# An ISAB attention with a SwiGLU feed-forward: a written list of block kinds, lent buffers and a listed opening

## Chip, cores and metric

The kernel runs on one core of one Trainium2 chip. The metric is device time in microseconds (us). TensorE, VectorE, ScalarE, GpSimd and SyncE are the engines; the profile calls them PE (its weight loads PEld), DVE, ACT, POOL and SP.

## What is computed

`x` has 4 batches of 12416 rows of 128 channels; there are 32 inducing points `I`.

```
mab(q, kv): softmax(q @ kv.T / sqrt(128)) @ kv
h  = mab(I, x)              # 32 rows for each batch
y  = mab(x, h)              # one row for each row of x
yn = y / rms(y) * rms_g
out = (silu(yn @ w_gate) * (yn @ w_val)) @ w_out      # 128 -> 1536 -> 128
```

Since `y = a @ h` with only 32 attention weights `a` for each row, the kernel never forms `y`. It multiplies `h` (scaled by `rms_g`) into the two first weight matrices once for each batch (the stacks `sg` and `sv`), and the rms norm follows from a 32 x 32 Gram matrix of `h`. The moving operand of the feed-forward part is `a`, split into a high and a low half so that a reduced-precision matmul (fp32r) loses nothing that matters: 4 x 32 rows fill the 128 partitions (high, low, high, low).

## The kernel before

**Tiling.** A batch is cut into 7 sets: five of 16 tiles of 128 rows, one of 15, one of 2. Set `s` has four units (quarters of its partitions), the last set one: 25 units to a batch, 20 of 512 columns, 4 of 480 and one of 256. A unit has 12 slots, one for each 128 of the 1536 hidden channels: 300 slots to a batch, 1200 in all.

**A slot** (`ffn.slot`, L674 to L701): a gate matmul (L677), Silu on ScalarE (L685), a value matmul (L688), their product on VectorE (L694). The product `u` then has to be multiplied with its piece of `w_out` and summed over the 12 slots. This is done in one of two ways.
- *plain*: one true fp32 matmul (`acc<-u,wo`, L613; it appears as two records).
- *three*: `u` is split into a high part, a scaled low part and their difference, and three fp32r matmuls (L633, L635, L613 with `more` or `xn` weights) take its place. There are two kinds. *sums*: one ScalarE (L659), one VectorE (L660) and one GpSimd operation (L669). *differences*: two ScalarE (L663, L668) and two GpSimd operations (L664, L669). Split tiles come from a ring of RING = 4 sets (`hi`, `lo`, `d`). The last two slots of a unit (j of 10 and 11) have no split weights and are always plain.

**Who decides.** The order on every engine is the order of the code: nothing is rescheduled. Before it emits the loop, the kernel rehearses it on a small model of its engines (`rehearse`). In `slot` of the rehearsal `decide` chooses the kind of each block by limits on how far an engine would fall behind in the next 8 slots (`fits`, LIMIT), and the filling of TensorE with ready projections is written down in `picks`. So each engine has one fixed order, and an instruction that waits holds everything behind it.

**Beside the slots** the next batch's attention is planned into slots (`schedule`): x loads, transposes, scores, softmax, weighted sums, stacks, second scores. A *seam* (L483) of 8 steps turns the attention weights of one set into `hi` and `lo` halves; `gather` (L537) copies them with DMAs from the SP queue into the moving tile `a` of a unit (4 DMAs of 64 KB).

**The opening** is written out by hand (L703 to L802). x and five of nine weight chunks are loaded; each weight chunk arrives as 64-bit floats and is rounded by `power`, `power_number`, `upper`, `upper_number`, `sign`, `lower` (VectorE, ScalarE, and one GpSimd multiply, after which a rounded `w_gate` or `w_val` chunk is stored to DRAM on SP, L221). Every x tile is transposed on TensorE (L313) and copied by ScalarE (L316), scored (L322, L326), and after a maximum over all sets (`max1` to `max3`) exponentiated (L355), transposed (L364) and summed (L378). Then come `divide`, `turn_h`, the scores of set 0, its softmax over rows, its seam and `spread`, which makes the moving tile of unit 0 on TensorE instead of by DMA, and the gathers of units 1 and 2. In the first 24 slots of batch 0, units 0 and 1 alternate in fours: slots 0 to 3 are unit 0, slots 4 to 7 unit 1. No three-way block is allowed in batch 0 before slot 26. `warm` (L183) emits TensorE fillers.

Of the kernel before, what the change touches and what calls it, by code (L numbers as in the profile page):

```python
# [23 lines left out]
def kernel(  # L24
# [73 lines left out]

    NK = NJ - 2
    RING, RESERVE, HELD, SILU = 4, 7, 9, 3  # L100

# [28 lines left out]
    def load_rows(b, s):  # L130

        n = per[s]
        t = xnat[b, s] = xnp.tile([P, 16 if b and n > 4 else n, C], F32, name=f"xn{s % 2 if b and n > 4 else s}")
        if b or s == full:
            for q in range(R):
                nc.sync.dma_start(out=t[ts(q, m), 0:n, :], in_=of(xrows, b, s)[q])
        else:
            d = xrows[ds(start[s], P * n), :].rearrange("(p t) c -> p t c", t=n)
            nc.sync.dma_start(out=t[:], in_=d)
# [34 lines left out]
    sel = up.tile([P, 512], F32R, name="u")[:, 0:2 * P].rearrange("p (k r c) -> p k r c", k=2, r=R)  # L174
    nc.gpsimd.memset(sel.bitcast(F32), 0.0)
    for k in range(R):
        nc.gpsimd.tensor_copy(out=sel[:, k % 2, k, :], in_=ident[:, 0:m])
# [36 lines left out]
    def rounding(i, c):  # L214
# [20 lines left out]
        def power():  # L235
# [12 lines left out]
            e = st["e"] = work.tile([P, 512], I32, name="we", tag="work")  # L248
# [25 lines left out]
        def lower():  # L274
            if wide:
                e, f = st["e"], st["f"].bitcast(F32)
                nc.vector.scalar_tensor_tensor(out=f[:], in0=st["low"].bitcast(U32), scalar=2.0 ** -52, in1=f[:],
                                               op0=ALU.mult, op1=ALU.add)
                nc.gpsimd.tensor_tensor(out=st["dst"], in0=f[:], in1=e.bitcast(F32)[:], op=ALU.mult)  # L279
            put()  # L280

# [8 lines left out]
    def attention(b, load_next):  # L290
# [9 lines left out]
        def turn_x(s, k):  # L300

            n = per[s]
            if b:
                t = xT[b, s]
                nc.vector.transpose(out=t[:, ts(k, n * m)], in_=t[:, ts(k, n * m)])
                return
            if not k:
                xT[b, s] = xtp.tile([P, R * n * m], F32, name=f"xT{s}")
            now = range(k * R, min(n, k * R + R))
            if now:  # L310
                ps = bank()
                for t in now:
                    nc.tensor.transpose(ps[:, ts(t - k * R, P)], xnat[b, s][:, t, :], ident[:])  # L313
                dst = xT[b, s][:].rearrange("p (q t i) -> p t q i", q=R, i=m)[:, now.start:now.stop, :, :]
                src = ps[:, 0:len(now) * P].rearrange("p (t q i) -> p t q i", q=R, i=m)
                nc.scalar.copy(out=dst, in_=src)  # L316
# [43 lines left out]
        def turn_e(s):  # L360
            e = st["e", s] = (once.tile([P, P], F32, name="hT") if b and per[s] < R else
                              work.tile([P, per[s] * m], F32, name="e", tag="work") if b else
                              up.tile([P, 512], F32, name="u"))[:, 0:per[s] * m]
            nc.vector.transpose(out=e, in_=sc[b][:, cols1[s]])  # L364

        def sum_h(*sets):

            hl = st["hl"]
            if b or not sets[0]:
                st["ps"] = bank()  # L370
            ps, whole = st["ps"], range(NS) if not b else sets
            tiles = [(s, t) for s in whole for t in range(per[s])]
# [6 lines left out]
            if b and sets[0]:  # L379
                nc.vector.tensor_tensor(out=hl[:, 0:C], in0=hl[:, 0:C], in1=ps[:, 0:C], op=ALU.add)  # L380
            elif b:
                nc.vector.tensor_copy(out=hl[:, 0:C], in_=ps[:, 0:C])
# [8 lines left out]
        def divide():  # L391
            st["hn"] = st["hl"][:, 0:C]
            nc.vector.tensor_scalar_mul(out=st["hn"], in0=st["hn"] if b else st["ps"][:, 0:C], scalar1=st["rl"][:])

        def turn_h():
# [5 lines left out]
            if b:  # L401
                scale_h()
# [5 lines left out]
        def square_h():  # L408

            if not b:  # L410
                scale_h()
# [3 lines left out]
            for q in range(R):  # L415
                to, of_ = gram[b][ts(q, m), ts(q, m)], ps[ts(q, m), 0:m]
                if b:
                    nc.vector.tensor_scalar_add(out=to, in0=of_, scalar1=C * 1e-6)
                else:
                    nc.scalar.activation(to, of_, AF.Copy, bias=C * 1e-6)  # L420

        def scores2(s, ps=None):
            ps = ps or scores(s, st["hT"][:, 0:m], quarters[s], per2[s])
# [40 lines left out]
        def stack_of(i, c):  # L464

            ps = st["stack", i, c] = bank()
            nc.tensor.matmul(ps[:], st["hg"][:], w0.pop((i, c)), start=True, stop=True)  # L467
            nc.scalar.copy(out=stacks[b][i][:, ts(c, 512)], in_=ps[:])
# [14 lines left out]
    def seam(b, s):  # L483

        st = {}
        n, rows = per2[s], rows2[s]
        w = n * m
        engine = nc.gpsimd if b or s else nc.vector
# [4 lines left out]
        def turn_a():  # L493
            eT = st["eT"] = work.tile([P, 512], F32, name="eT", tag="work")
            nc.vector.transpose(out=eT[rows, 0:w], in_=sc[b][rows, cols2[s]])
# [4 lines left out]

        def turn_z():
            ps = st["ps"]
            z = st["z"] = work.tile([P, n, m], F32, name="z", tag="work")
            flat = z[rows, :, :].rearrange("p t m -> p (t m)")
            nc.vector.tensor_tensor(out=flat, in0=ps[rows, 0:w], in1=st["eT"][rows, 0:w], op=ALU.mult)
            nc.vector.transpose(out=flat, in_=flat)

        def scale():
            ms = numbers("ms")
            nc.vector.reduce_sum(out=ms, in_=st["z"][rows, :, :], axis=AX.X)  # L510
            nc.vector.tensor_scalar(out=ms, in0=ms, scalar1=1.0 / C, scalar2=1e-6, op0=ALU.mult, op1=ALU.max)  # L511
            st["ms"] = ms
# [5 lines left out]
        def apply():  # L518
            rs, a = st["rs"], weights(b, s)
            engine.tensor_tensor(out=a, in0=a, in1=rs.unsqueeze(2).to_broadcast((rs.shape[0], n, m)), op=ALU.mult)  # L520

        def turn_b():
            aT = st["aT"] = work.tile([P, 512], F32, name="aT", tag="work")
            nc.vector.transpose(out=aT[rows, 0:w], in_=sc[b][rows, cols2[s]])

        def split():
            aT = st["aT"]
            hi, lo = split_of[b, s] = [halves.tile([P, 512], F32R, name=k) for k in ("hi", "lo")]
            if b or s:
                nc.scalar.copy(out=hi[rows, 0:w], in_=aT[rows, 0:w])  # L530
            else:
                nc.vector.tensor_copy(out=hi[rows, 0:w], in_=aT[rows, 0:w])
            engine.tensor_tensor(out=lo[rows, 0:w], in0=aT[rows, 0:w], in1=hi[rows, 0:w].bitcast(F32), op=ALU.subtract)

        return [turn_a, square, turn_z, scale, root, apply, turn_b, split]

    def gather(b, u):  # L537

        s, q = units[u]
        w = per2[s] * m  # L540
        hi, lo = split_of[b, s]
        a = moving[b, u] = (xnp.tile([P, 512], F32R, name="xn0") if (b, u) == (0, 2) else
                            astk.tile([P, 512], F32R, name="a"))
        for k, half in enumerate((hi, lo, hi, lo)):
            nc.sync.dma_start(out=a[ts(k, m), 0:w].bitcast(F32), in_=half[ts(q, m), 0:w].bitcast(F32))

    def spread(b, u):

        s, q = units[u]
        w = per2[s] * m  # L550
        hi, lo = split_of[b, s]
        assert not q and not flowing
        ps = bank()
        for k, half in enumerate((hi, lo)):
            nc.tensor.matmul(ps[:, 0:w], sel[:, k, :, :].rearrange("p k m -> p (k m)"), half[:, 0:w],
                             start=not k, stop=bool(k))
        a = moving[b, u] = astk.tile([P, 512], F32R, name="a")
        nc.scalar.copy(out=a[:, 0:w], in_=ps[:, 0:w])
# [7 lines left out]
    def split_wo(step):  # L566

        if not step:
            kws["first"] = xnp.tile([P, half + NK, C], F32R, name=f"xn{full - 1}")
            for name in ("hi", "lo", "d"):  # L570
                kws[name] = xnp.tile([P, RING, 512], F32R, name=f"xn{full - 4 + len(kws) - 2}")
# [23 lines left out]

    def weight_of(kind, j):
        n = kind * NK + j
        return kws["first"][:, n, :] if n < half + NK else kws["more"][:, n - half - NK, :]

    def ffn(b, u):  # L600
# [28 lines left out]
        def project3(j, hi, lo, d):  # L629
            if st["k"] == nk:  # L630
                st["u"] = ps_u.tile([P, 512], F32, name="u3")
            ups = st["u"]
            nc.tensor.matmul(ups[:, 0:T], weight_of(0, j), hi, start=st["k"] == nk, stop=False)  # L633
# [6 lines left out]
            kws["out"] -= 1  # L640

        def store(o):
            if s == full:
                d = out[ds(b * N + start[s], P * per[s]), :].rearrange("(i w) c -> i w c", i=m)
            else:
                d = of(out, b, s)[q]
            for k in range(R):
                queue = nc.scalar if (b, u) == flat[-1] and k % 2 else nc.sync
                queue.dma_start(out=d[:, :, ts(k, m)], in_=o[ts(k, m), 0:T].rearrange("p (t c) -> p t c", c=m))

        def three(j, t):

            assert kws.get("out", 0) < RING
            kws["out"] = kws.get("out", 0) + 1
            n = kws["n"] = (kws.get("n", 0) + 1) % RING
            hi, lo, d = (kws[name][:, n, 0:T] for name in ("hi", "lo", "d"))
# [9 lines left out]
            def rest():  # L666
# [3 lines left out]
                kara.append(lambda: project3(j, hi, lo, d))  # L670
# [41 lines left out]
    def parts(i, c, *engine):  # L712
        one = weight[i, c]
        one["power"]()
        one["power_number"](*engine)
        one["upper"]()
        one["upper_number"](*engine)

    def join(i, c):
        weight[i, c]["sign"]()  # L720
        weight[i, c]["lower"]()

    f["open_"]()
    warm(6)
    for s in range(NS):
        for k in range(R):
            f["turn_x"](s, k)

        for one in {0: (0,), 3: (1, 2), 4: (3, 4), NS - 1: (NS - 2,)}.get(s, ()):
            f["scores1"](one)  # L730
        if s == 4:
            parts(0, 0, nc.vector)
        if s == 5:
            join(0, 0)
    f["scores1"](NS - 1)
    one = weight[1, 0]
    f["max1"]()
    one["power"]()
    warm(4)
# [459 lines left out]
```

## Time and profile before

| | us |
|---|---|
| three runs | 1622.79, 1622.80, 1623.58 |
| profiled run, span | 1621.7 |
| L669, GpSimd, 705 operations | 870.9 |
| L664, GpSimd, 139 operations | 178.6 |
| L613 plain, TensorE, 990 records | 490.8 |
| first gate matmul starts | 55.48 |

The page gives the busy time of each engine, the chain that ended last, and the costliest groups of instructions. In a timeline a line is the start, the duration, the engine, the source line and operation, the tiles (written `<-` read), the shape and the number of instructions that were merged; in square brackets stands the idle time before and what ended it. Matmuls are pipelined: their durations overlap, and the distance between two starts is what one costs.

Two things about the opening are read from the timeline of VectorE: from 20 us on it is busy most of the time, and the weights' rounding stands in the same queue as the attention chain. The last loads of x land at about 22 us.

### The profile page before, as it was taken

What the parts mean: (1) busy time and instruction counts of PE and PEld (TensorE: products, weight loads), DVE (VectorE), ACT (ScalarE), POOL (GpSimd) and SP (SyncE); (2) the same over time, 40 slices, a digit from 0 to 9 for tenths busy, and PEclk for the clock granted to TensorE, in tenths of its full rate; (3) what the DMA queues carried; (4) which work ended last, traced back from release to release, by engine and by line L of the source; (5) the groups of instructions that cost most, each with busy time, mean ns of one, the idle gap of its engine ahead of it and who ended that gap; (6) DMA issues with size and microseconds to landing.
All of it is one profiled execution on the core that took longest, in us unless ns stands there. A gap on an engine that the chain in (4) does not pass through costs nothing.

```text
span 1621.7 us, 25435 instructions
## 1 busy us (share of the span) xinstructions
PE 1604.3 (99%) x7085; PEld 1085.6 (67%) x7085; DVE 1444.6 (89%) x2504; ACT 1238.3 (76%) x2285; POOL 1217.7 (75%) x979
## 2 busy tenths in 40 slices
PE   8999999999999999999999999999999999999998
PEld 6546666756676666766677666676667777777776
DVE  4879988999899998899899998789989999999997
ACT  4567877767887778776778777877778888878886
POOL 1358885878588886688678888587858878878876
PEclk9999999999999999999999999999999999999999
DMA  7455624444353141634445323353221122111221
GB/s 262 91 72 85 112 43 97 88 97 69 60 94 59 36 95 29 133 76 81 69 67 83 55 54 68 63 125 79 46 38 29 31 39 40 35 35 36 40 38 26
DMA packets 389181, 112.52 MB, mean 69 GB/s; under 512 B 365072, under 2 KB 369712, under 8 KB 386480
## 3 DMA queue, kind: packets, MB, share of 16 engines
q1 hardware_dynamic: 388304, 110.82, 34.8%
q8 instruction: 56, 0.92, 0.3%
q14 instruction: 85, 0.70, 0.2%
q10 hardware_dynamic: 736, 0.08, 0.0%
HBM read 53.95 MB, written 27.00 MB: 50 GB/s over the span
## 4 chain that ended last, share of the span: by engine, by line
PE 94%; DVE 1%; ACT 1%; issue 1%; POOL 0%; DVEq 0%; ACTq 0%
PE acc L613 35%; PE gv L677 18%; PE gv L688 16%; PE u L635 10%; PE u L633 10%; PE gv L322 3%; PE gv L499 1%; PE gv L378 1%; DVE gv L694 1%; ACT silu L685 1%; PE gv L453 0%; DVE xn L660 0%; PE gv L467 0%; DVE o L621 0%; POOL xn L279 0%
## 5 line engine op out<-in xcount | busy, mean ns | idle before, releaser
L669 POOL TENSOR_TENSOR xn<-xn,xn 128x512 fp32r<-128x512 f32 (+2 forms) x705 | 870.9, 1255 | 268.6 <-DVE xn L660 156.8
L685 ACT ACTIVATE silu<-gv 128x512 f32<-128x512 f32 (+2 forms) x1186 | 689.7, 586 | 258.4 <-PE gv L677 231.8
L688 PE MATMUL gv<-a,sv 128*128 128x512 f32 (+2 forms) x1188 | 636.1, 536 | 0.8 <-ACT silu L685 0.8
L613 PE MATMUL acc<-u,wo 128*128 128x512 f32 (+1 forms) x990 | 490.8, 581 | 0.0
L677 PE MATMUL gv<-a,sg 128*128 128x512 f32 (+2 forms) x1188 | 486.7, 410 | 1.5 <-ACT silu L685 0.8
L694 DVE TENSOR_TENSOR u<-silu,gv 128x512 f32<-128x512 f32 (+2 forms) x621 | 407.7, 663 | 51.7 <-PE gv L688 32.3
L694 DVE TENSOR_TENSOR gv<-silu,gv 128x512 f32<-128x512 f32 (+2 forms) x565 | 376.0, 668 | 66.1 <-PE gv L688 49.0
L660 DVE SCALAR_TENSOR_TENSOR xn<-xn,gv 128x512 fp32r<-128x512 f32 (+2 forms) x566 | 371.3, 656 | 9.5 <-ACT xn L659 5.9
L659 ACT ACTIVATE xn<-gv 128x512 fp32r<-128x512 f32 (+2 forms) x566 | 330.4, 584 | 43.1 <-DVE gv L694 30.9
L677 PEld LDWEIGHTS gv<-a,sg 128*128 128x128 f32 x1188 | 223.8, 188 | 189.4 <-ACT silu L685 40.2
L688 PEld LDWEIGHTS gv<-a,sv 128*128 128x128 f32 x1188 | 223.6, 188 | 139.6 <-issue 46.3
L613 PE MATMUL acc<-xn,more 128*128 128x512 f32 (+2 forms) x705 | 273.6, 388 | 3.0 <-DVE o L621 2.6
L633 PE MATMUL u<-xn,xn 128*128 128x512 f32 (+2 forms) x705 | 272.4, 386 | 0.0
L613 PEld LDWEIGHTS acc<-u,wo 128*128 128x128 f32 x990 | 184.9, 188 | 46.7 <-issue 9.1
L664 POOL TENSOR_TENSOR xn<-u,xn 128x512 fp32r<-128x512 f32 (+2 forms) x139 | 178.6, 1285 | 41.6 <-ACT xn L663 41.6
L635 PE MATMUL u<-xn,xn 128*128 128x512 f32 (+2 forms) x414 | 160.1, 387 | 0.0
L613 PEld LDWEIGHTS acc<-xn,more 128*128 128x128 f32 x705 | 132.4, 188 | 33.5 <-POOL xn L669 5.7
L633 PEld LDWEIGHTS u<-xn,xn 128*128 128x128 f32 x705 | 132.6, 188 | 28.6 <-issue 5.5
L663 ACT ACTIVATE xn<-u 128x512 fp32r<-128x512 f32 (+2 forms) x139 | 87.4, 629 | 36.6 <-DVE u L694 32.4
L635 PE MATMUL u<-xn,more 128*128 128x512 f32 (+2 forms) x291 | 112.5, 387 | 0.0
L516 POOL TENSOR_TENSOR rs<-ms,mhalf 128x16 f32<-128x16 f32 (+2 forms) x28 | 75.9, 2709 | 18.1 <-DVE ms L511 17.1
L635 PEld LDWEIGHTS u<-xn,xn 128*128 128x128 f32 x414 | 77.7, 188 | 17.5 <-DVE gv L694 0.2
(151 smaller groups left out, 1096.9 us busy)
## 6 DMA issues: line engine op xcount, KB each, us to landing
out_dram<-o SPq DMA_DIRECT2D x320, 64.0 KB, 2.0
xT<-in_x_dram SPq DMA_DIRECT2D x60, 256.0 KB, 5.4
xn<-in_x_dram SPq DMA_DIRECT2D x60, 256.0 KB, 5.0
a<-hi SPq DMA_DIRECT2D x156, 64.0 KB, 2.0
a<-lo SPq DMA_DIRECT2D x156, 64.0 KB, 2.0
xn<-in_x_dram SPq DMA_DIRECT2D x5, 1024.0 KB, 10.6
xn<-w SPq DMA_DIRECT2D x18, 256.0 KB, 3.6
out_dram<-o SPq DMA_DIRECT2D x64, 60.0 KB, 2.0
```

The lines of the kernel that those rows point to most:

```text
L613: nc.tensor.matmul(acc[:, 0:T], lhsT, rhs, start=st["left"] == NJ, stop=st["left"] == 1)
L633: nc.tensor.matmul(ups[:, 0:T], weight_of(0, j), hi, start=st["k"] == nk, stop=False)
L635: nc.tensor.matmul(ups[:, 0:T], weight_of(1, j), lo, start=False, stop=not st["k"])
L659: nc.scalar.activation(hi, v, AF.Copy, scale=(1.0 - 2.0 ** -13) * 2.0 ** -12)
L660: nc.vector.scalar_tensor_tensor(out=lo, in0=hi.bitcast(F32), scalar=-4096.0, in1=v, op0=ALU.mult, op1=ALU.add)
L663: nc.scalar.activation(d, v, AF.Copy, scale=1.0 - 2.0 ** -13)
L664: nc.gpsimd.tensor_tensor(out=lo, in0=v, in1=d.bitcast(F32), op=ALU.subtract)
L669: nc.gpsimd.tensor_tensor(out=d, in0=hi.bitcast(F32), in1=lo.bitcast(F32), op=ALU.subtract)
L677: nc.tensor.matmul(g[:, 0:T], sg[:, ts(j, P)], a[:, 0:T], start=True, stop=True)
L685: nc.scalar.activation(sl[:, 0:T], g[:, 0:T], AF.Silu)
L688: nc.tensor.matmul(v[:, 0:T], sv[:, ts(j, P)], a[:, 0:T], start=True, stop=True)
L694: nc.vector.tensor_tensor(out=t[:, 0:T], in0=sl[:, 0:T], in1=v[:, 0:T], op=ALU.mult)
```

## The change

1. **Kinds of blocks.** `decide`, `fits`, LIMIT and the table of loads go. The kinds stand in a list of 900 letters (`s`, `d`, `.`), 300 each for batch 0, for batches 1 and 2 together, and for batch 3. In batch 3 slots 10 and 11 may be three-way as well: `split_last` makes their split weights in the buffer `xT0`.
2. **Lent buffers.** The ring of four sets becomes a list of free sets, and two more sets are cut out of the second pair of stack buffers (`sg`, `sv`), which is idle between two batches: lent at slot 20 (batch 0) or 2, called back at slot 184, gone at 192. In batch 3 they stay.
3. **Some prices** of the rehearsal change (for instance `sum_h` 1.85 to 2.0), and it knows when the accumulator bank of an older unit is free.
4. **The opening** is cut into some 200 named steps that stand in one listed order. The softmax of the inducing points over the rows of x has three groups of sets with a maximum each, (0,1,2), (3,4), (5,6); their sums are brought together by factors exp(difference of maxima). Six of the copies of transposed x go to VectorE. The load of set 5 is cut in two DMAs.
5. **Set 0 in two halves.** The scores are split into halves of 8 row tiles. The seam of the first half is in the opening, that of the second is planned into slots 5 to 15. Units 0 and 1 are now made of the first half of all four quarters and units 2 and 3 of the second, so a gather for these is 8 DMAs of 32 KB and a store 8 instead of 4. Of the gathers only that of unit 1 stays in the opening; that of unit 2 goes to slot 18. The weight chunks (0,1) and (1,1) are finished in the opening, at the end of the list, ahead of the gather.

The core of the diff:

```diff
+    GROUPS = ((0, 1, 2), (3, 4), (5, 6))
+    HALF = 8
+    ORDER = """
+        tx03 cp03v tx00 tx02 tx01 cp00 cp01 cp02v sc0 tx12 tx13 tx10 cp12v cp13v tx11 ev0 tx23 cp11v tx21 tx60 cp10
...
+        te5 rec pn10 p11 su4 shs dv0 su5 sg20 dv1 su6 dv2 th lw20 hT sg10 s2A gp gr0 hg tnA gr2 rmxA subA gr3 s2B w6
+        jn20 lw10 pn11 e2A ta u01 gr1 sq tnB z jn10 so00 tz rz ms rmxB ca00 so10 w12 un01 u11 sl00 subB pow ap un11
+        ca10 e2B silu tb hi sp1 lo sl10 sg01 sg11 sp2 cpa lw01 jn01 gate lw11 jn11
+    """
+    LENT = (RING, RING + 1)
...
+    def lend(b, k, idle, leaving):
+
+        if k == (20 if not b else 2):
+            idle += LENT
+            return True
+        if b + 1 < B and k == 184:
+            leaving += [n for n in LENT if n not in idle]
+            idle[:] = [n for n in idle if n not in LENT]
+        assert k != 192 or not leaving
...
+    def lend_tiles():
+
+        tiles = [stk.tile([P, F], F32R, name=name) for name in ("sg", "sv")]
+        kws["sets"][RING:] = [[t[:, ts(n, 512)] for n in range(3)] for t in tiles]
...
     gather(0, 1)
-    gather(0, 2)
-    weight[0, 1]["lower"]()
     flowing.append(True)
...
-            add(0, weight[1, 1]["sign"])
-            add(1, weight[1, 1]["lower"])
-            for k, one in ((1, (2, 1)), (5, (0, 2)), (8, (1, 2)), (11, (2, 2))):
+            for k, one in ((0, (2, 1)), (5, (0, 2)), (8, (1, 2)), (11, (2, 2))):
...
+            for k, step in zip((5, 6, 8, 9, 10, 13, 14, 15), seam(0, 0, 1)):
+                add(k, step)
+            add(18, gather, 0, 2)
...
+        if b + 1 == B:
+            for step in range(3):
+                add(2 + 2 * step, split_last, step)
...
-    LIMIT = (0, 0.8, 0.8, 2.6)
     kinds, picks = {}, {}
+    letters = """
+        ..........................d....dsd...d..s.dd.s..dss.ssdssd..dssssddd.d..ss..dsdd....dsds.d.ss...sds.
...
+    BLOCKS = [letters[NU * NJ * n:NU * NJ * (n + 1)] for n in (0, 1, 1, 2)]
...
-            kind = decide(b, k, u, j)
+            kind = {"s": "sums", "d": "differences"}.get(BLOCKS[b][k])
```

In the list, the letters name a step and the digits its set or weight chunk: `tx`/`cp` transpose and copy (a final `v`: on VectorE), `sc`/`ev` scores and their eviction, `m1` to `m3` the maximum, `ex`/`te`/`su` exponential, transposition and sum, `dv` the division, `th`/`hT` the transposed `h`, `s2`, `tn`, `rmx`, `sub`, `e2` the scores and softmax of a half (A, B), `ta` to `lo` the seam of the first half, `sp` and `cpa` the spread, `w` fillers; `p`, `pn`, `u`, `un`, `sg`, `lw`, `jn` the rounding of a weight chunk, `so`, `ca`, `sl` a stack.

## The prediction

> **What bounds the kernel now.** I read the page first (busy shares, chain of work that ended last), then the timeline of TensorE in the steady part, then the chain in order of time, and last the timeline around the first matmul of the feed-forward part.
>
> ```profile
> PE 1604.3 (99%) x7085; PEld 1085.6 (67%) x7085; DVE 1444.6 (89%) x2504; ACT 1238.3 (76%) x2285; POOL 1217.7 (75%) x979
> PE 94%; DVE 1%; ACT 1%; issue 1%; POOL 0%; DVEq 0%; ACTq 0%
> ```
>
> TensorE is busy almost throughout and is 94% of the chain. A busy TensorE need not be a full one, so I price its work by the distance between starts:
>
> ```profile
> 331.99 0.40 PE L677 MATMUL gv<-a,sg 128*128 128x512 f32 x1
> 332.22 1.02 PE L613 MATMUL acc<-u,wo 128*128 128x512 f32 x2
> 332.68 0.79 PE L688 MATMUL gv<-a,sv 128*128 128x512 f32 x1
> 333.31 0.40 PE L677 MATMUL gv<-a,sg 128*128 128x512 f32 x1
> 333.54 0.40 PE L633 MATMUL u<-xn,xn 128*128 128x512 f32 x1
> 333.78 0.39 PE L635 MATMUL u<-xn,xn 128*128 128x512 f32 x1
> 334.01 0.39 PE L613 MATMUL acc<-xn,more 128*128 128x512 f32 x1
> 334.24 0.40 PE L688 MATMUL gv<-a,sv 128*128 128x512 f32 x1
> ```
>
> Gate to gate with one plain fp32 projection is 333.31 − 331.99 = 1.32 us. A reduced matmul takes 0.23, so plain costs 1.32 − 2 x 0.23 = 0.86. The same projection as three reduced matmuls takes 334.24 − 333.54 = 0.70. Converting a block of 512 columns therefore saves TensorE 0.16 us; of 480 columns 0.15 and of 256 about 0.08, in proportion.
>
> With these prices the work after the opening is: gate and value matmuls 960, 192 and 48 pairs (512, 480, 256 columns), 542 us; 705 three-way blocks (567, 105, 33), 476; 495 plain ones, 414; attention inside the loop about 96 (the rows of L322, L378, L453, L499, L467). Together 1528 us, against 1561 from the first gate matmul at 55.48 to the last projection at about 1616.9. So about **33 us are gaps**. One batch repeats every 394.1 us (first lines of the second scores of the next batch, chain in order of time):
>
> ```profile
> 334.63 0.99 PE gv L322 x8
> ...
> 728.77 0.99 PE gv L322 x8
> ...
> 1122.95 1.00 PE gv L322 x8
> ```
>
> The opening is another regime: TensorE runs fillers (L183) and a chain over VectorE, ScalarE and GpSimd sets the start:
>
> ```profile
> 53.55 0.62 SPq L545 DMA_DIRECT2D a<-hi  x1
> 53.55 0.69 DVE L533 TENSOR_TENSOR lo<-aT,hi 128x512 fp32r<-128x512 f32 x1
> 55.47 0.58 SPq L545 DMA_DIRECT2D a<-lo  x1
> 55.48 0.50 PE L677 MATMUL gv<-a,sg 128*128 128x512 f32 x1
> 58.69 0.53 SPq L221 DMA_DIRECT2D w<-xn  x1
> 59.51 0.39 PE L677 MATMUL gv<-a,sg 128*128 128x512 f32 x1
> ```
>
> Unit 0 starts at 55.48, 1.24 us after `lo` is finished at 54.24. Unit 1 starts with slot 4 at 59.51; its four gathers had been issued by 56.05 and, at 2.0 us to landing, were there at about 57.5. The store of the rounded weight chunk (L221) stands behind them in SP's queue.
>
> **What the skill says.** *FP8 and Floating Point Precision*, TensorE Precision Notes: true fp32 takes four passes, reduced fp32 reads 4 bytes and truncates. The trace agrees: 0.86 is nearly four times 0.23. *SBUF — State Buffer*, Who interferes with whom: VectorE and GpSimd share one port pair, and a VectorE instruction with two SBUF inputs or in a 2-port mode blocks. The trace agrees in the opening: L249 at 44.42 took 0.90 us beside GpSimd's multiply (43.77, 1.27 us), and 0.43 at 50.15. In the steady part VectorE's L694 and L660 have one operand in PSUM, so by that page they leave the pair alone. *GPSIMD Engine Reference*, Engine selection, puts two-input elementwise work at about twice VectorE's time; here 1.29 (L533 on GpSimd, 512 columns) against 0.69.
>
> **Part 1: the list of kinds.** The letters hold 556 sums and 230 differences, 786 three-way blocks, against 566 + 139 = 705. By width: 634, 114, 38 against 567, 105, 33. Saving on TensorE: 67 x 0.1625 + 9 x 0.15 + 5 x 0.08 = **12.7 us**; the engine bounds, so it goes to the end. The price is paid elsewhere. GpSimd gets 81 + 91 = 172 more operations; from the row `3.56 us x3` at 799.06 one 480-column operation repeats every 1.17, so 1.25 at 512: about +207 us. ScalarE gets 91 x 2 x 0.63 − 10 x 0.58 = +108, VectorE −10 x 0.66. GpSimd goes to about 1430 of 1605 (89%), ScalarE to 84%, VectorE stays at 90%. All below TensorE on average, so I charge nothing to the sum, but dense units exceed it: unit 5 of batch 0 (9 blocks, 5 differences) asks 14 x 1.25 = 17.5 us of GpSimd in about 14.4 of TensorE. The two lent sets (six instead of four) let that queue up. Their effect on gaps is not visible before: bounded by −10 (batches 0 to 2 come down to the 1.2% of gap that I count in batch 3) and +10 (a wait of 0.013 us per block). I take −3, since six sets make the waits for a free one rarer. The three small weight splits of the last batch (3 ScalarE operations at 0.38 and 2 GpSimd at 0.73, by the 256-column rows of L659 and L669) hide beside its slots.
>
> **Part 2: the opening.** The last x set lands at 22.1 (issued 4.5, 17.6 to landing), in both. Before, its chain waits for one maximum over all sets (bias at 29.8), four exponentials (to 33.7), transposes (to 36.3). After, only sets 5 and 6 are left then. VectorE, in order, decides. Its queue from the first copy at 8.8 to the last score eviction holds 17 us, and that eviction's data come at about 26: end at 26 to 28.7, say 27.5. From there the listed order gives: 24 instructions to `hT` (transposes 0.65, two-input 0.60, tensor_scalar in SBUF 0.34, small ones 0.12 to 0.35) 8.0; sign, scaling and the scores of the half set 0.9; the half chain (256-column steps 0.44 each as in 1572.96 to 1573.39, lw10, u01, tnB, then a power of 8 columns, 1.63 by the 32x8 row of L516, under which rmxB, u11, sl00, subB lie) to the end of `lo` 7.9; two port locks by the multiplies jn20 and jn10, 0.9 each. `lo` ends at 27.5 + 18.6 = **46**, the first gate at 47.3: 8.2 earlier.
>
> But not all of that is kept. The built order shows on SP, ahead of the gathers of unit 1: the store of jn01, a raw load, the store of jn11. After `lo` VectorE does sl10, sg01, sg11, lw01, lw11 (5 x 0.61), GpSimd jn01 and jn11 (1.28 each, the first behind lw11 by the port): jn11 ends at `lo` + 5.7. Then the store (0.53), then **eight** gathers of half width at 0.63 apart (as 53.55 to 58.00 shows) instead of four: last issue at + 10.7, landing 1.8 later: + 12.5, about 58.5. Slot 4 needs it and TensorE's order is fixed, so TensorE stands from about + 6 to + 12.5. Slot 4 starts at 58.5 against 59.51: **1 us earlier, not 8**. VectorE has caught up by then (before, slot 4's product ran at 62.88, 3.4 after its gate; now 0.9 after), but gets the second half's seam in slots 5 to 15 (0.42 + 0.79 + 0.54 + 0.42 = 2.2, GpSimd 2.9, ScalarE 0.35, TensorE 0.05). I take −2 for the opening, bounds −8 (the gathers don't hold) and +1.
>
> **Part 3: the end.** The last unit has differences up to slot 9; the chain of two ScalarE and two GpSimd steps (0.4 and 0.73 at 256 columns) is partly beside the last plain products: +0.3.
>
> **Sum.** 1621.7 − 12.7 − 3 − 2 + 0.3 = 1604.3; the other runs lie 1.1 above the profiled span (1622.8): **1605**.
>
> **Rivals.**
> 1. The gathers of unit 1 don't hold slot 4 (they land in time or other work fills in): the opening keeps its 8.2, and 1622.8 − 12.7 − 3 − 8.2 + 0.3 = **1599**. For it: slots 0 to 3 need jn01 as well (their weight product so01), so slot 4 may be late whatever the gathers do, and only the difference counts; against it: one in-order queue and the issue times above. 19%.
> 2. GpSimd's higher share turns into waits at the reduced projections: gaps grow by 6 instead of falling by 3, **1614**. For it: dense units above 100%. Against it: six sets, and only 5.7 us of waits of weight loads on L669 now. 20%.
> 3. GpSimd becomes the bound: **slower**. All its work after 75 us is 982 block operations (in units of 512) x 1.25 + 157 = 1385 us, which ends at 1460. If port conflicts made one operation cost more than 1.42, it would end at 1625 or later; at 1.43, **1636**. Against it: the median is 1.287, the maximum 1.330. 8%.
> 4. The gain of part 1 is eaten exactly: 1623. 3%.
> My own case, 50%, spans 1599 to 1611. A measurement tells about 0.2% from no change. The range takes in rivals 1 and 2: 1593 to 1617. Faster 0.89, same 0.03, slower 0.08.
>
> **What would show it.** Right: 786 three-way blocks; about 390 us from batch 1 to 2; the first gate near 47; a TensorE idle of about 6 us before the gate of slot 4, released by a DMA; gaps about 30. Wrong: slot 4 at 52 with no wait (rival 1); weight loads waiting long on the GpSimd subtraction (rivals 2, 3); VectorE much later than 46 with `lo`, for which I counted port locks only twice.

## The result and the profile after

The changed kernel takes **1640.5 us** (median of 4 runs, 1639.5 to 1641.8) against 1622.8: a ratio of 1.0108, 95% interval 1.0096 to 1.0120. It is slower, and the forecast was 1605. From the page of the changed kernel, its busy times, its chain by engine and its clock row (PEclk, the TensorE clock that was granted, in tenths of full speed):

```profile
PE 1595.6 (97%) x7100; PEld 1092.9 (67%) x7100; DVE 1458.7 (89%) x2519; ACT 1301.2 (79%) x2457; POOL 1425.9 (87%) x1160
PE 86%; DVE 4%; ACT 3%; DMA 2%; issue 2%; POOL 1%; SPq 1%; POOLq 0%; DVEq 0%; ACTq 0%
PEclk8899999999999999999999999999999999999999
```

GpSimd's 1425.9 us are the 1430 that the forecast worked out. TensorE's share of the chain fell from 94% to 86%, and its clock row now begins with two slices below the rest. The chain in order of time shows where the loss is not (first lines of the second scores of the next batch):

```profile
351.69 1.00 PE gv L332 x8
...
746.44 1.00 PE gv L332 x8
...
1142.31 1.00 PE gv L332 x8
```

A batch takes 394.8 and 395.9 us, no less than before (394.1 and 394.2); 390 had been forecast. But the first of these lines stands 17.1 us later than before. So two things need an explanation: an opening that loses some 18 us, and 81 more three-way blocks that bring next to nothing.

The timeline of the opening, TensorE first:

```profile
21.81 2.37 PE L804 MATMUL gv<-ident,xn 128*128 128x128 f32 x10 [8.77 <-DMA xn<-in_x_dram]
51.98 0.67 PE L506 MATMUL gv<-eT,gram 128*128 128x256 f32 x2 [3.23 <-DVE eT L502]
59.87 0.50 PE L750 MATMUL gv<-a,sg 128*128 128x512 f32 x1 [0.68 <-ACT a L591]
71.14 0.76 PE L750 MATMUL gv<-a,sg 128*128 128x512 f32 x1 [5.83 <-DMA a<-lo]
71.70 1.91 PE L685 MATMUL acc<-u,wo 128*128 128x512 f32 x2
72.62 1.41 PE L761 MATMUL gv<-a,sv 128*128 128x512 f32 x1
```

TensorE stands 8.8 us for an x load, 3.2 for VectorE's `eT`, and 5.8 for a gather. The first gate is at 59.87 (before 55.48), the one of slot 4 at 71.14 (before 59.51). After the stand a pass of a plain projection takes 72.62 − 71.70 = 0.92 us, where it took 332.68 − 332.22 = 0.46 in the steady part. The Trainium skill, *TensorE: Matmul & The Clock Gate*, Part 1, says that an idle array falls to half its clock until it has been busy for a few microseconds; the factor of two after a stand of 5.83 us agrees. The window from 71 to 77 us (busy us of TensorE, its weight loads, VectorE, ScalarE and GpSimd with their instruction counts; then the clock as a share of full speed, the DMA share, GB/s) has it directly, a clock of 0.52:

```profile
71.00:77.00 6.00, 5.86 (x10) 3.01 (x10) 1.29 (x2) 1.68 (x3) 0.00 (x0) 0.52 0.90 135
```

VectorE in the same stretch:

```profile
25.97 0.69 DVE L816 TENSOR_SCALAR_CACHE_REDUCE sc<-gv 128x512 f32<-128x512 f32 x1 [12.61 <-PE gv L332]
37.23 0.66 DVE L816 TENSOR_SCALAR_CACHE_REDUCE sc<-gv 128x480 f32<-128x480 f32 x1 [0.41 <-PE gv L332]
50.79 0.69 DVE L293 SCALAR_TENSOR_TENSOR o<-sc,o 128x512 f32<-128x512 uint32 x1 [2.08 <-DMA sc<-in_moe_w_gate_dram]
51.76 1.35 DVE L278 TENSOR_SCALAR o<-sg 128x512 int32<-128x512 int32 x1
58.01 0.43 DVE L552 TENSOR_TENSOR lo<-aT,hi 128x256 fp32r<-128x256 f32 x1
74.14 0.69 DVE L767 TENSOR_TENSOR u<-silu,gv 128x512 f32<-128x512 f32 x1 [6.25 <-PE gv L761]
```

It is idle for 12.6 us behind TensorE's stand and waits 2.1 us for a raw weight chunk at `lw10` (L293). The two port locks that the forecast counted are there (L287 at 45.54 and L278 last 1.71 and 1.35, beside GpSimd's multiplies). The last score eviction (480 columns, set 5) ends at 37.9 and not at 27.5, `lo` at 58.44 and not at 46. While TensorE stands for the gather, VectorE has nothing left to do and waits 6.25 us.

SyncE's queue (SPq) between `lo` and slot 4:

```profile
62.84 0.33 SPq L236 DMA_DIRECT2D w<-xn  x1
63.26 0.38 SPq L224 DMA_DIRECT2D sg<-in_moe_w_out_dram  x1
64.26 0.33 SPq L236 DMA_DIRECT2D w<-xn  x1
64.64 0.62 SPq L577 DMA_DIRECT2D a<-hi  x1
...
69.11 0.59 SPq L577 DMA_DIRECT2D a<-lo  x1
```

This is what the forecast described: store, raw load, store, eight gathers. Slot 4 starts at `lo` + 12.7; + 12.5 had been forecast, with a stand of about 6 before it where 5.83 is seen.

The following table is worked out from the timelines of TensorE: the start of the n-th gate matmul less that of the kernel before, in us, and the same for the end of the span. All later sections use it. Each row is one profiled run and can differ from the medians: that of the mended opening took 1621.3 us, 1.3 above its median, that of the kernel before 1623.6, 0.8 above.

| kernel | gate 0 | 4 | 26 | 200 | 300 | 600 | 900 | end |
|---|---|---|---|---|---|---|---|---|
| after | 4.4 | 11.6 | 18.6 | 17.1 | 17.5 | 19.5 | 20.1 | 18.3 |
| new opening, kinds of before | 4.9 | 12.1 | 19.3 | 20.9 | 21.2 | 23.3 | 25.2 | 25.6 |
| set 6 last | −5.9 | 1.3 | 8.6 | 7.0 | 7.6 | 8.5 | 9.3 | 7.4 |
| gather first | 5.8 | 7.3 | 11.5 | 9.9 | 10.4 | 11.2 | 11.9 | 9.3 |
| mended opening | −7.6 | −6.1 | −0.3 | −1.8 | −1.3 | −0.4 | 0.3 | −2.2 |
| + gather of unit 2 earlier | −8.4 | −7.0 | −4.5 | −6.0 | −5.2 | −4.3 | −3.7 | −6.2 |
| + places earlier | −8.1 | −6.6 | −4.2 | −5.8 | −5.1 | −6.3 | −7.6 | −9.1 |
| new kinds, old opening | −0.9 | −0.9 | −0.9 | −2.4 | −1.7 | −2.1 | −2.6 | −5.2 |
| new kinds in the last batch only, old opening | −0.9 | −0.9 | −1.0 | 2.4 | 2.6 | 5.0 | 7.2 | 5.4 |
| new kinds, GpSimd narrow | −0.6 | −0.6 | −0.6 | −2.0 | −1.2 | −4.3 | −7.5 | −10.0 |
| new kinds, VectorE narrow | −0.7 | −0.7 | −0.7 | −2.1 | −1.3 | −4.4 | −7.7 | −10.2 |

### The profile page after: what moved, and what is told of

The parts are those of the page before. It is cut to its first block, busy times and chain, and to the rows that moved or that the text cites. A ratio compares the mean times of both kernels' runs of the same rounds, so it can differ in the third digit from the quotient of the medians.

```text
span 1640.0 us, 25981 instructions
## 1 busy us (share of the span) xinstructions
PE 1595.6 (97%) x7100; PEld 1092.9 (67%) x7100; DVE 1458.7 (89%) x2519; ACT 1301.2 (79%) x2457; POOL 1425.9 (87%) x1160
## 4 chain that ended last, share of the span: by engine, by line
PE 86%; DVE 4%; ACT 3%; DMA 2%; issue 2%; POOL 1%; SPq 1%; POOLq 0%; DVEq 0%; ACTq 0%
PE acc L685 28%; PE gv L750 16%; PE gv L761 15%; PE u L708 10%; PE u L706 10%; PE gv L332 3%; DMA xn<-in_x_dram 1%; PE gv L506 1%; PE gv L384 1%; DVE u L767 1%; ACT silu L758 1%; DVE gv L767 1%; SPq L577 1%; ACT xn L732 1%; DVE xn L733 0%
## 5 line engine op out<-in xcount | busy, mean ns | idle before, releaser
L742 POOL TENSOR_TENSOR xn<-xn,xn 128x512 fp32r<-128x512 f32 (+2 forms) x602 | 741.1, 1249 | 80.2 <-DVE xn L733 33.5
L685 PE MATMUL acc<-u,wo 128*128 128x512 f32 (+2 forms) x828 | 414.3, 584 | 0.5 <-DVE u L767 0.5
L732 ACT ACTIVATE xn<-gv 128x512 fp32r<-128x512 f32 (+2 forms) x428 | 249.8, 584 | 62.3 <-DVE gv L767 51.4
L733 DVE SCALAR_TENSOR_TENSOR xn<-xn,gv 128x512 fp32r<-128x512 f32 (+2 forms) x428 | 281.1, 657 | 11.0 <-ACT xn L732 6.0
L737 POOL TENSOR_TENSOR xn<-u,xn 128x512 fp32r<-128x512 f32 (+2 forms) x174 | 217.9, 1252 | 14.0 <-ACT xn L736 13.9
L706 PE MATMUL u<-xn,xn 128*128 128x512 f32 (+2 forms) x578 | 224.8, 389 | 0.0
L685 PE MATMUL acc<-xn,more 128*128 128x512 f32 (+2 forms) x578 | 223.5, 387 | 0.5 <-POOL xn L742 0.4
L742 POOL TENSOR_TENSOR sg<-sg 128x512 fp32r<-128x512 f32 (+1 forms) x92 | 118.0, 1282 | 8.2 <-DVE sg L733 2.8
L706 PEld LDWEIGHTS u<-xn,xn 128*128 128x128 f32 x578 | 108.7, 188 | 23.6 <-issue 4.9
L742 POOL TENSOR_TENSOR sv<-sv 128x512 fp32r<-128x512 f32 (+2 forms) x92 | 117.5, 1277 | 7.2 <-DVE sv L733 3.1
L708 PE MATMUL u<-xn,xn 128*128 128x512 f32 (+2 forms) x286 | 109.9, 384 | 0.0
## 6 DMA issues: line engine op xcount, KB each, us to landing
xn<-in_x_dram SPq DMA_DIRECT2D x5, 1024.0 KB, 10.2
```

Source lines behind the costliest of these rows:

```text
L685: nc.tensor.matmul(acc[:, 0:T], lhsT, rhs, start=st["left"] == NJ, stop=st["left"] == 1)
L708: nc.tensor.matmul(ups[:, 0:T], weight_of(1, j), lo, start=False, stop=not st["k"])
L732: nc.scalar.activation(hi, v, AF.Copy, scale=(1.0 - 2.0 ** -13) * 2.0 ** -12)
L733: nc.vector.scalar_tensor_tensor(out=lo, in0=hi.bitcast(F32), scalar=-4096.0, in1=v, op0=ALU.mult, op1=ALU.add)
L737: nc.gpsimd.tensor_tensor(out=lo, in0=v, in1=d.bitcast(F32), op=ALU.subtract)
L742: nc.gpsimd.tensor_tensor(out=d, in0=hi.bitcast(F32), in1=lo.bitcast(F32), op=ALU.subtract)
```

## The experiments

All ran beside the kernel before, at 1623.1 to 1623.5 us. Line numbers of the variants can differ by a few from those of the changed kernel.

**The changed kernel with the kinds of the kernel before**, that is, with the new opening, the new planner and the lent sets.

```diff
     letters = """
-        ..........................d....dsd...d..s.dd.s..dss.ssdssd..dssssddd.d..ss..dsdd....dsds.d.ss...sds.
...
+        ..........................s.....s.....d.ss.d.d..sssdssds.s..sdd.sd......dsssd..ssd..sdssds.ds...sdsd
...
```

> The changed kernel with the kinds of the kernel before (705 three-way blocks) in its list; opening, halves and lent sets stay. Theory A (the opening carries the loss, 17 us by the second scores of batch 0, and the kinds are a wash): 1638 to 1642 us. Theory B (the opening costs only the 11.6 us seen at slot 4, the denser kinds the rest): about 1634. Theory C (my forecast of the kinds holds, 12 us saved): about 1652.

Measured: 1649.8 us, 1.0166 (1.0151 to 1.0181). With all else left as it is, the new kinds are worth 9.3 us (1649.8 against 1640.5). This is not the opening alone: by the table 19.3 us are lost at gate 26, and 5.9 more up to gate 900, where the kinds of before lose time under the new planner with the old opening as well (below).

**The kinds alone: the kernel before with the list of kinds, lent sets, new prices and the split of the last weights.**

```diff
+    LENT = (RING, RING + 1)
...
-            kind = decide(b, k, u, j)
+            kind = {"s": "sums", "d": "differences"}.get(BLOCKS[b][k])
```

> The kernel before with the list of kinds, the lent sets, the new prices and the split weights of the last batch, but the old opening and whole sets. Theory A (wash): 1621 to 1624 us. Theory B (denser kinds cost): about 1629. Theory C (saved TensorE time reaches the end, as forecast): 1607 to 1611.

Measured: **1618.8 us**, 0.9975 (0.9965 to 0.9985): 4.3 us faster than before, below the range of theory A and far from C. Put on top of these kinds, the new opening costs 1640.5 − 1618.8 = 21.7 us, more than the whole loss.

**The gather of unit 1 right behind `lo`**, ahead of the stores and the raw load on SyncE's queue.

```diff
-        ca10 e2B silu tb hi sp1 lo sl10 sg01 sg11 sp2 cpa lw01 jn01 gate lw11 jn11
+        ca10 e2B silu tb hi sp1 lo ga1 sl10 sg01 sg11 sp2 cpa lw01 jn01 gate lw11 jn11
...
-    gather(0, 1)
```

> The changed kernel with the eight gathers of unit 1 issued right after the low half, ahead of the two weight stores on SP. Queue theory: the last gather lands at lo + 6.8 us instead of lo + 12.5, slot 4 starts about 5.5 us earlier (near 65.5), time about 1635. Rival (slot 4 is held by the weight rounding anyway): slot 4 near 70, time 1639 to 1641.

Measured: 1634.3 us, 1.0070 (1.0055 to 1.0085). Slot 4 is at 66.79 and waits for no DMA. 6.2 us are won, as the theory of the queue has it; the first gate itself moves from 59.87 to 61.30.

**Set 6 last**: its transposes, copies, scores and eviction behind those of set 5.

```diff
-        ... tx23 cp11v tx21 tx60 cp10 tx20 ... ev1 cp60 sc2 tx33 p00 sc6 pn00 ev6 ev2 ...
+        ... tx52 tx53 tx60 te1 cp52 m21 m2r1 jn00 p01 cp53 cp60 m2s1 u10 sc5 sc6 ev5 ev6 m3p1 ...
```

> The changed kernel with the transposes, copies, scores and eviction of set 6 moved behind those of set 5 in the list, as set 6 is loaded last. Order theory: TensorE no longer stands 8.8 us for set 6, the first gate comes 5 to 8 us earlier (52 to 55) and so does the end, 1632 to 1635. Rival (sets 2 and 3 land that late themselves): first gate near 59, 1640.

Measured: 1629.8 us, 1.0041 (1.0027 to 1.0055): 10.7 won, more than forecast. Set 6 is loaded by the last four x DMAs (issued from 9.50 on), and the list used it before set 2 was complete. TensorE's timeline of this kernel:

```profile
60.82 0.77 PE L751 MATMUL gv<-a,sg 128*128 128x512 f32 x1 [5.83 <-DMA a<-lo]
```

The first gate is at 49.5, near the forecast 47.3, and slot 4 still waits 5.83 us for the gather: the two faults are independent.

**The low words ahead of the next raw load, alone.** `jn20` fetches the next raw chunk into the place whose low words `lw10` has not yet read, so that `lw10` waits for that load (and then, by the code, takes the low words of the other chunk; it multiplies them by 2^-52, so at most about 2^-20 of a weight).

```diff
-        jn20 lw10 pn11 e2A ...
+        lw10 jn20 pn11 e2A ...
```

> The changed kernel (1640.5 us) with one mend of the three alone: lw10 ahead of jn20, so that VectorE doesn't wait for the next raw chunk. Theory (the delay of 2.1 us on VectorE, and the 3.2 us that TensorE then waits for eT, lie on the chain to lo): 1637 to 1638.5. Rival (slot 4 waits for its gather whatever comes before): 1640 to 1641.

Measured: 1638.4 us, 1.0091 (1.0076 to 1.0106): 2.1 us won, slot 4 at 69.45.

**All three mends.**

> The changed kernel with three mends in its opening: set 6 treated behind set 5 in the list, the gather of unit 1 issued right behind lo, and lw10 ahead of jn20. Theory A (the opening lost its time by the order of its list alone): first gate about 49, slot 4 at 53 to 55 without a wait for a DMA, and slot 26 near 93, which is where the kernel with the old opening and the new kinds has it, so 1617 to 1620 us. Theory B (what was won in the first half is given back by the second half of the set, which is made in the slots: VectorE's sums late, the gather of unit 2 late, the clock low after the stand): slot 26 at 97 or later, 1623 to 1628.

Measured: **1620.0 us**, 0.9982 (0.9973 to 0.9990): 20.5 won, against 10.7 + 6.2 + 2.1 one by one. The first gate is at 47.92 (forecast: 47.3), slot 4 at 53.41 without a wait. The total and gate 26 (93.62, where 93 had been expected) are those of theory A. But the 7.6 us of lead at gate 0 are down to 0.3 at gate 26, as theory B has it in kind. A window of this kernel (columns as above) and TensorE's lines at the two longest of its waits:

```profile
48.00:60.00 12.00, 10.48 (x32) 5.92 (x33) 11.64 (x20) 6.81 (x12) 4.43 (x4) 1.00 0.68 151
```

```profile
51.12 1.13 PE L467 MATMUL gv<-xn,hg 128*128 128x512 f32 x2 [1.51 <-POOL xn L299]
88.13 0.52 PE L751 MATMUL gv<-xn,sg 128*128 128x512 f32 x1 [1.92 <-DMA xn<-lo]
88.44 1.91 PE L686 MATMUL acc<-u,wo 128*128 128x512 f32 x2
89.37 1.42 PE L762 MATMUL gv<-xn,sv 128*128 128x512 f32 x1
```

Without the stand VectorE is busy 11.64 of the first 12 us, above all with the rounding of weight chunks and the products of the slots. The waits that TensorE's timeline names before gate 26 are 1.51 us for GpSimd's product of a rounded weight chunk (`jn01`, which follows VectorE's `lw01`), 1.03 for a product of VectorE, 0.57 for a second chunk, and 1.92 for the gather of unit 2, after which TensorE runs at half clock (0.93 us a pass). How much a less busy VectorE would bring here was not tried.

**The gather of unit 2 two slots earlier**, on top of the mended opening.

```diff
-            add(18, gather, 0, 2)
+            add(16, gather, 0, 2)
```

> The kernel with the mended opening (1620.0 us), with the gather of unit 2 issued in slot 16 and not in slot 18. Theory Q (its eight transfers stand on the synchronization engine's queue behind loads for the next batch, so that slot 24 waits 1.9 us for them and TensorE then starts at a low clock): slot 24 without a wait, 1616.5 to 1618. Rival (VectorE, which is full from 46 to 79 us, sets slot 24 anyway): 1619.5 to 1620.5.

Measured: 1617.6 us, 0.9964 (0.9951 to 0.9977). 2.4 us won. The wait at slot 24 is 0.21; in the profiled runs gate 26 comes 4.2 us sooner and the end 4.0.

**The end: kinds of the last 24 slots as before**, with the mended and with the old opening.

> The same with the kinds of the last 24 slots as before. Theory: the differences in the last unit cost 2.7 us behind the last value matmul, so 2 to 3 us less than the run with the mended opening. Rival (they also saved TensorE time ahead of the end, so that nothing is won): the same within 0.7.

> The old opening, the new kinds and lent sets, but the kinds of the last 24 slots as before. Theory (tail worth 2.7 us): 1616 to 1617 us against 1618.8 with the new last letters. Rival (tail worth nothing): 1618 to 1619.5.

Measured: 1620.8 us, 0.9983 (0.9976 to 0.9990), and 1619.8 us, 0.9978 (0.9970 to 0.9987), against 1620.0 and 1618.8. The theory falls. In the changed kernel the stretch behind the last gate matmul is 2.6 us longer than before (9.9 against 7.3), but the ten slots ahead of it are 2.6 shorter (8.4 against 11.1): work changed places.

**New kinds in the last batch only**, the first three with the kinds of before (old opening).

> The old opening, the lent sets and new prices, the new kinds only in the last batch (without its last 24 slots), and the kinds of before in the first three batches. Theory G (in the first three batches the saving of TensorE is eaten by gaps, since the waits grow as GpSimd and ScalarE come closer to their limits): within 2 us of the run with new kinds in all batches, 1616 to 1619. Theory S (each of the 63 more three-way blocks in those batches saves its 0.157 us): 10 us slower than that run, 1625 to 1627.

Measured: 1628.9 us, 1.0033 (1.0021 to 1.0044). Ten us slower than with new kinds everywhere, the difference that theory S named (the time itself is above its range), but also 5.6 slower than the kernel before, which no theory said: with the kinds of before in three batches and the last batch's saving, about 2.8 us less than the kernel before would be expected. So the ten us are not the saving of 63 blocks alone, and their agreement with S is in part luck. By the table the kernel loses 8.2 us between gates 26 and 900. Of this, 6.1 are lost at one place in each batch, beside the exponentials (slots 140 to 150: 3.1, 1.5 and 1.5 us by the same difference); the kernel with new kinds everywhere loses nothing there. TensorE there in the first batch, and behind the same two waits in the second:

```profile
248.37 0.50 PE L716 MATMUL gv<-a,sg 128*128 128x512 f32 x1 [0.30 <-DVE u L730]
249.55 0.49 PE L727 MATMUL gv<-a,sv 128*128 128x512 f32 x1 [0.68 <-ACT silu L724]
250.38 3.38 PE L653 MATMUL acc<-u,wo 128*128 128x512 f32 x4
252.77 1.41 PE L727 MATMUL gv<-a,sv 128*128 128x512 f32 x1
...
647.79 0.50 PE L727 MATMUL gv<-a,sv 128*128 128x512 f32 x1 [0.69 <-ACT silu L724]
...
648.62 1.88 PE L653 MATMUL acc<-u,wo 128*128 128x512 f32 x4
649.94 0.80 PE L727 MATMUL gv<-a,sv 128*128 128x512 f32 x1
```

**Narrow work for three engines in the middle batches** (old opening, new kinds; TensorE's work and all orders the same). For the blocks whose factors stand in one of the four old sets, an engine works on 128 of the 512 columns; the other 384 keep what an earlier block left there.

```diff
-                nc.gpsimd.tensor_tensor(out=d, in0=hi.bitcast(F32), ...
+                h = 128 if b in (1, 2) and where < RING else T
+                nc.gpsimd.tensor_tensor(out=d[:, 0:h], in0=hi[:, 0:h].bitcast(F32), ...
```

and likewise for `lo` on GpSimd, for the ScalarE copies, or for VectorE's `lo`.

> The old opening with the new kinds (1618.8 us), but in the two middle batches GpSimd's instructions for a three-way block in one of the four old sets work on 128 of 512 columns; the rest of these factors is left as an earlier block wrote it. The order of all instructions is the same. Theory G (the saving of the middle batches, 3 us each, is lost because GpSimd is full there): 1612.5 to 1615 us. Theory A (ScalarE's copies are what is late) and theory V (VectorE): 1617.5 to 1619.

> The same, but ScalarE's instructions for these blocks work on 128 of 512 columns, and GpSimd's on all. Theory A: 1612.5 to 1615 us. Theories G and V: 1617.5 to 1619.

> The same, but VectorE's instruction for the sums kind in these blocks works on 128 of 512 columns. Theory V: 1612.5 to 1615 us. Theories G and A: 1617.5 to 1619.

Measured: 1613.7 us, 0.9943 (0.9928 to 0.9958); 1616.8, 0.9961 (0.9947 to 0.9976); 1613.7, 0.9942 (0.9927 to 0.9957). GpSimd and VectorE each give 5 us back, ScalarE 2. The windows over the two middle batches (columns as above), first the kernel with the new kinds, then GpSimd narrow, then VectorE narrow:

```profile
340.00:1110.00 770.00, 763.44 (x3385) 520.98 (x3385) 697.27 (x1194) 629.74 (x1193) 705.31 (x568) 1.00 0.39 73
```

```profile
340.00:1110.00 770.00, 766.23 (x3403) 524.97 (x3402) 694.80 (x1204) 632.64 (x1199) 461.80 (x573) 1.00 0.39 73
```

```profile
340.00:1110.00 770.00, 765.40 (x3405) 526.43 (x3405) 647.02 (x1205) 634.24 (x1200) 710.71 (x572) 1.00 0.39 73
```

GpSimd was relieved of 243 us in one case, VectorE of 50 in the other, and the effect is the same. So GpSimd as the one full engine, theory G as it was put, falls. Between gates 300 and 900 the new kinds gain 0.9 us, with GpSimd narrow 6.3, with VectorE narrow 6.4; 44 blocks at the forecast's 0.157 would be 6.9. So either brings back nearly all that is missing there. Both engines are above 90% busy in that stretch (705 and 697 of 770), and a block's factors pass through two or three engines in turn, so a shorter step could bring them to TensorE sooner; but that reading is argued and not shown. ScalarE, relieved of 79 us, gives only 2, and the same narrowing was not tried on the kernel before, whose gaps of 33 us might shrink too.

**Every third block of the differences kind plain again in the middle batches.**

> The old opening with the new kinds (1618.8 us), but in the two middle batches every third block of the differences kind is plain again: 40 fewer three-way blocks in all, 51 us less GpSimd work in each of the two batches. Theory G (VectorE and GpSimd are so full there that the last blocks bring no net time): 1617.5 to 1620. Theory S (each block saves its 0.157 us): 1625.

Measured: 1624.8 us, 1.0008 (0.9999 to 1.0017): 5.9 us slower for 40 blocks fewer, 0.148 us a block. Theory S: a block there is worth nearly its TensorE time, and taking GpSimd work away in this form brings nothing back.

**Nothing lent.**

```diff
     def lend(b, k, idle, leaving):
+        return False
```

> The old opening with the new kinds, but with four sets of factors throughout: nothing is lent. Theory (the new kinds make more factors at once than four sets hold, so that TensorE takes blocks early and waits for them): 1622 to 1628 us against 1618.8. Rival (four sets would do): 1618 to 1620.

Measured: 1643.7 us, 1.0127 (1.0111 to 1.0142): 25 us slower, far more than forecast. These kinds cannot do with four sets.

**The planner's prices as before, and its bank rule out as well.**

```diff
-            "sum_h": (2.0, .25), "scores2": (1.19, .63), "square": (1.02,),
+            "sum_h": (1.85, .25), "scores2": (1.07, .63), "square": (.87,),
...
         def bank_of(unit):
+            return 0.0
```

> The old opening with the new kinds (1618.8 us), the planner's nine raised TensorE prices as before. Theory P (the 8 us that the middle of the kernel lost beside the saved passes come from another order of queued blocks under the new prices, as in the run with the kinds of before in three batches, which was 5.6 us slower than the kernel before): 1612 to 1616. Theory N (the places where TensorE runs out of work come with the new kinds themselves): 1617.5 to 1621.

> The same, and the planner's new rule left out by which a unit's first block waits for its bank. Theory P': if this rule and the prices together lost the 8 us, 1611 to 1615. Theory N: 1617.5 to 1621. If the rule saves waits of TensorE for VectorE's last sums, this is slower than the run with the old prices alone by 1 to 3.

Measured: 1620.2 us, 0.9982 (0.9975 to 0.9989), and 1619.2 us, 0.9975 (0.9965 to 0.9985), against 1618.8. With the new kinds neither is the cause (theory N); with the kinds of before they were not tried.

**The second stack of the next batch two slots earlier**, on top of the mended opening and the earlier gather.

```diff
-                add(197 + 7 * i, g["stack"], i)
+                add(197 + 5 * i, g["stack"], i)
...
-                    add(199 + 7 * i + k, g["place"], i, k)
+                    add(199 + 5 * i + k, g["place"], i, k)
```

> The kernel with the mended opening and the gather of unit 2 in slot 16 (1617.6 us), with the second stack of the next batch (its product and the placing of its halves) two slots earlier, at slots 202 to 207. Theory (z waits up to 2.2 us for a buffer that a transfer into sv still reads; the transfer stands behind gathers and a store on the synchronization engine's queue, and TensorE then runs at a low clock): without this wait in two batches 2 to 3 us less, 1614.5 to 1616. Rival (the wait moves to another place, since the queue carries the same transfers): 1617 to 1619.

Measured: **1614.5 us**, 0.9946 (0.9929 to 0.9962), 3.1 less than without: faster than the kernel before and than the changed one. The wait that it takes away looks like this in the changed kernel, where TensorE then waits 0.57 us for `z` and 0.70 for the product behind it:

```profile
766.36 0.66 DVE L511 TENSOR_TENSOR z<-gv,eT 128x480 f32<-128x480 f32 x1 [2.19 <-DMA sv<-whi]
```

`z` needs the buffer that a transfer out of `whi` still reads, and half of those transfers stand behind a unit's gathers and the stores of an output on SyncE's queue. The wait comes with the new kinds: `z` waits for these transfers 2.2 us in all in the kernel with the new kinds alone and 3.6 in the changed one, and never in the kernel before or in the two runs that have the kinds of before in the first three batches.

Every compute engine of this last kernel has as many instructions as in the changed one, in another order.

## Why the prediction was wrong

**Part 2, the opening: the failed step is "end at 26 to 28.7, say 27.5" for the last score eviction, and all that was counted from it.** It took VectorE's queue as running from 8.8 us on, whatever TensorE did. The list puts set 6 between transposes of set 2, while its load is issued last; TensorE's order is fixed, so it stood until 21.8 and VectorE until 25.97, and the last eviction ended at 37.9, 10.4 late. The step compared the last load with the last consumer, and not each consumer in the list with its own load. By experiment it is 10.7 us. From the eviction to the end of `lo` 18.6 us were forecast and 20.5 measured: the raw load in front of `lw10`, which the forecast counted in the half chain without a wait, held VectorE for 2.08 and is worth 2.1 by experiment. With both and the gather mended the last eviction ends at 28.4, `lo` at 46.7, and the first gate is at 47.92, where 27.5, 46 and 47.3 had been worked out: the sums of instructions were right, the waits were missed.

**The gathers behind the stores** were forecast to a quarter of a microsecond (12.7 after `lo` against 12.5) and are worth 6.2 by experiment. Rival 1 is refuted.

**What came behind slot 4** is the second part of the opening's error: the forecast took −2 for the whole opening from slot 4 being 1 us early, but from gate 4 to gate 26 the changed kernel loses 7.0 us more (11.6 to 18.6). "VectorE has caught up by then" held, since VectorE waited 6.25 us during the stand. Missed were the half clock after the stand (6 us at a clock of 0.52, by estimate 6 x 0.48 = 2.9 us lost), the gather of unit 2, whose move to slot 18 was described and not priced (a wait of 1.84 at slot 24), and waits of 1.03 for VectorE and 0.57 for GpSimd. In the mended opening the lead of 7.6 us is gone in the same stretch, and 4.2 of it come back with the earlier gather.

**Part 1, the kinds.** The saving on TensorE of 12.7 us (the sum as written comes to 12.64) is supported: 0.148 us a block by the thinner list, where 0.157 was used. The failed term is "I take −3" for the gaps. From gate 0 to the end the new kinds alone gained 5.2 − 0.9 = 4.3 in the profiles, so the gaps grew by 12.7 − 4.3 = 8.4 (by the medians 0.9 more), inside the bounds (−10 to +10) and at their other end. They grew in the first three batches only: from gate 900 to the end the gain is 2.6, close to the 18 blocks x 0.157 = 2.8 of the last batch, which has no attention beside it. Rival 2 came near in size (+6) but gave it to GpSimd alone. ScalarE's busy time rose by 63 us and not by 108.

Shown: narrowing VectorE's or GpSimd's part in two of the three batches brings 5 back; the wait of `z`, which comes with the new kinds, is worth 3 in the mended kernel; the planner's prices and bank rule are nothing with these kinds; fewer blocks are no cure. Open: why the gaps grew. Between gates 26 and 900 the new kinds gain 1.7 us where 63 blocks x 0.157 = 9.9 were due, so 8.2 are missing. The kinds of before, under the new planner with lent sets, lose 8.2 there as well, but most of it beside the exponentials, where the new kinds lose nothing; so one cause in the planner for both is neither shown nor excluded. Lending alone was not tried with the kinds of before.

**Rival 3**, GpSimd as the bound, is refuted: its operation on 512 columns takes 1.29 us in the mean, far from the 1.42 that the rival needed, and it waits for others still. The slower side came by a mechanism that no rival named, an order of consumers that didn't follow the order of the loads. **Part 3**, +0.3 for the end, is not contradicted by the two runs on it.

## What to carry to other kernels

In a hand-written order, set each instruction's place against the landing of its own operand, engine by engine, and do the same for every DMA queued behind another's semaphore: here three misplaced entries cost 20 us and five moves took the same instructions from 1640.5 to 1614.5. An earlier first result is worth only what the waits of the next stage leave of it: here a lead of 7.6 us was 0.3 some 45 us later. When converting work to relieve the bounding engine, price also the waits that the preparing work may bring, not only its load: here a single block was worth nearly its saving, and yet the gaps took two thirds of the sum, with a cause that is only in part known.

## What was not expected of the hardware

TensorE can lose clock after stands much shorter than the idle window of about 3.4 us that the Trainium skill names (*TensorE: Matmul & The Clock Gate*, Part 1). In the kernel with new kinds in the last batch only, named waits of 0.30 and 0.68 us within 1.2 us were followed by four plain passes in 252.77 − 250.38 = 2.39 us. In the second batch the same two waits, 0.29 and 0.69, left the clock alone: the four passes took 649.94 − 648.62 = 1.32, and the place lost 1.5 us instead of 3.1. Nor did the wait of 1.51 us in the mended opening lower the clock (1.00 from 48 to 60 us). So a short wait can cost more than itself, here 1.1 us on four passes, but need not. Over the twelve runs of the mended opening time and mean clock go together: 1621.0 to 1621.5 us at 0.997 and 0.998, 1618.9 to 1620.1 at 0.999 and 1.000.

Issues of gathers on SyncE's queue stand 0.64 us apart, whether one moves 64 KB (53.55 to 58.00 before, seven steps) or 32 (64.64 to 69.11 after), so cutting four gathers into eight half as large doubled their time on the queue from 2.5 to 5.1 us.
